# Four attention layers on one core: seven exponential buffers, key tiles of 512, and a new order of the side work

## The chip, the core and the metric

The kernel runs on one core of one Trainium2 chip. The metric is the device time of one execution in microseconds (us). Five engines work side by side, each through its own instructions in a fixed order: TensorE (PE in the profile, its weight loads apart as PEld) multiplies matrices into PSUM, ScalarE (ACT) computes the exponentials, VectorE (DVE) and GpSimd (POOL) do elementwise work, and SyncE (SP) issues the DMA transfers. Engines wait for each other by semaphores.

## What is computed

Four residual layers over x of 2048 rows and 512 columns, with 32 heads of 16 columns. Layers 0 and 2 see a window of 256 keys, layers 1 and 3 see all 2048 keys.

```python
qkv = (layernorm(x) @ wqkv).reshape(B, S, 3, H, Dh)      # H = 32, Dh = 16, S = 2048
scores = einsum("bhqd,bhkd->bhqk", q, k) * Dh ** -0.5     # window layers: 0 <= q - k < 256, else -1e9
o = einsum("bhqk,bhkd->bhqd", softmax(scores), v)
x = x + o.reshape(B, S, D) @ wo                           # A (window), B (full), A, B
```

## The kernel before

**Attention.** A layer is cut into four chunks of 512 queries (index `c`) and eight groups of four heads (`qd`, called a quad here). In a full layer a quad walks over 16 tiles `j` of 128 keys, and each tile is done in two halves `pr` of two heads: 32 steps to a quad, 1,024 to a full layer. A step is one call of `exps` (L748): eight matmuls of scores into one of two PSUM tiles `s` (L758), and one ScalarE exponential of 128x1024 numbers into a tile `e` from a pool of `EB` = 6 buffers (L762, L763). What the exponentials are multiplied with comes later: `attn_full` (L795) hands out closures `pv`, two for each `j`, each of 16 matmuls with the values into the accumulators `acc` (L808). Both closures of a `j` read both of its `e` tiles, so the two tiles come free when the second closure is done. `flush(n)` (L766) issues closures until only `n` are left; L801 sets how far they lag:

```python
flush(2 - pr + (1 if n == 3 or 12 <= n < 20 else 2 if 4 <= n < 12 else 0))
```

`n` is the step in the quad. The lag is longer at the start of a quad, since the accumulators have first to be emptied by DVE's two transposes of `epilogue` (L723, L726). The call of `flush` stands behind `exps` in each step, and so do its matmuls in TensorE's order.

**Side work.** Projections of keys and queries for later layers or chunks, values, and output projections are written as generators, wrapped in `Work` objects, and fed into the steps by `Side.share` (L975). TensorE's order is exactly the order in which the program issues; nothing reorders it later. The planner keeps a clock of its own (`spent`, `clock`), a time `PH["free"]` before which no side unit may go on, and a budget for each step. In full layers a side unit is a run of `mms` (L421): up to 12 pairs of 64-row matmuls into the one PSUM pair `PH["pair"]`, a piece to a step as a rule. Side.one (L927) picks the first work in the queue that is ready.

**Squares' sums.** After a projection of keys or queries (`keys` L577, `queries` L589) DVE joins the two PSUM halves and splits the result (L451, L452, L542, L543), POOL squares it (L548), and TensorE sums the squares by heads (`squares`, L568); DVE takes the maximum (L586) for keys or makes a row `m` for queries (L599, L600), and `m` goes to DRAM (L613), to the query tiles that are loaded later (L776). The TensorE part is put off: it is appended to `pend` with a due time 3.6 us later on the planner's clock. But in a full layer `mms` settles all of `pend` whenever the next unit begins, due or not (L424 to L427). At the end of each chunk `settle()` (L1046) does the same.

**Layer 3** is done in four passes `t` of two quads, each over the four chunks: 16 sections of 64 steps. `side3(t, c)` (L1182) lists what is done beside a section: the next chunk's queries of this pass (`Q3`), the next pass's keys of this chunk (`K3`), the output projection of the section before (`O3`), parts of the values (`upper`); in the last section of a pass also `shift3` (the key maximum of the next pass, which settles `pend` and writes a row of the keys) and the next pass's first queries. `Side.finish` (L986) issues what is left at the section's end without steps between.

**Loads.** `load_full` (L772) brings the next quad's queries `qt` (2 buffers) and its keys as two tiles `kt` of 1024 keys (3 buffers); `load_win` (L784) does it for the window layers. The schedule of every engine but TensorE is made at build time from priorities and from when a buffer should come free.

Of the kernel before, what the change touches and what calls it, by code (L numbers as in the profile page):

```python
# [31 lines left out]
MM = 0.222  # L32
HEAD_START = 100
HQ = QC // 2
EB, XB, XNB, WB, VB, OB = 6, 4, 4, 2, 3, 5
L_MIN = 2.0 ** -90
L_SUM = 2.0 ** 60

# [149 lines left out]
def fast_path(ctx, tc, flag, a_x, a_wqkv, a_wo, b_wqkv, b_wo, out):  # L188
# [214 lines left out]
    def phase(l):  # L403

        PH["full"], PH["win"] = l is not None and l % 2 == 1, l is not None and l % 2 == 0
        if PH["full"] or not PH["win"] and "pool" not in PH or l is None and PH.get("pair"):
            ps_x.close()
            PH["pool"] = ps_x.enter_context(tc.tile_pool(name=f"ps_x{l}", bufs=1 if PH["full"] else 2, space=bass.MemoryType.PSUM))
            PH["room"] = 0.0
            PH["pair"] = PH["pool"].tile([P, 2, QC], F32, name=f"s{l}") if PH["full"] else None  # L410

    def bank(halves=False):
# [5 lines left out]
            return ps_s.tile([P, 2, QC], F32, name=f"bs{turn['bank']}", tag="s")[:, 0, :]  # L418
        return PH["pool"].tile([P, QC], F32, name=f"b{turn['bank']}", tag="b")

    def mms(ps, pairs, after=1.6, us=MM):  # L421


        if PH["full"] and pend:  # L424
            settle()
            PH["free"] = clock[0] + 2.2
            yield 0.1  # L427
        for i, (a, b) in enumerate(pairs):
            if PH["full"]:
                for g in range(0, P, 32):  # L430
                    for r in range(2):
                        half = slice(R * r, R * r + R)
                        nc.tensor.matmul(ps[g:g + 32, r], a[half, g:g + 32], b[half], start=(i == 0),  # L433
                                         stop=(i == len(pairs) - 1), skip_group_check=True)
            else:
                nc.tensor.matmul(ps, a, b, start=(i == 0), stop=(i == len(pairs) - 1))  # L436
            spent(us)
            if i < len(pairs) - 1:
                if PH["full"]:
                    yield us  # L440
            else:
                PH["free"] = clock[0] + (1.7 if PH["full"] else after)
    TERMS = ((0, 0), (0, 1), (1, 0))

    def joined(n, ps, rows=slice(0, P)):
# [66 lines left out]
    def project(l, s, c, act, ht=None, first=None):  # L512


        ty, n = l % 2, f"{l}_{s}_{c}" + ("" if ht is None else f"_h{ht}")
        if not first:
            w = weights(ty, s, n, *((0, D) if ht is None else (ht * P, (ht + 1) * P)))
            yield wait(8)
            xc = XC[l, c]
        if s == 0:  # L520
            dst = rows(qs[ty, c])
        elif ty == 0:
            dst = rows(kw[c])
        else:
            dst = rows(kf)[:, :, c * QC:(c + 1) * QC]
        sqs = {}
        for t in range(NHT) if ht is None else (ht,):
            ps = bank(True)
            w0 = t * P if ht is None else 0
            if first:  # L530
                yield from mms(ps, [(first[0][:, k, t * P:(t + 1) * P], first[1][:, k, :]) for k in range(NC)])
            else:
                yield from mms(ps, [(w[:, k, a, w0:w0 + P], xc[:, b, k, :]) for k in range(NC) for a, b in TERMS], 2.2)
            settle(not sqs)
            ps = joined(f"{n}_{t}", ps)
            sp = vp.tile([P, 2, QC], F16, name=f"sp{n}_{t}", tag="sp", bufs=3)
            e = first[2][:, t:t + 1] if first else es[:, ty, s, t:t + 1]
            with tc.high_priority(HEAD_START):
                if act:
                    nc.scalar.activation(sp[:, 0], ps, AF.Copy, scale=e)  # L540
                else:
                    nc.vector.tensor_scalar(sp[:, 0], ps, e, None, op0=ALU.mult)  # L542
                nc.vector.scalar_tensor_tensor(sp[:, 1], ps, e, sp[:, 0], op0=ALU.mult, op1=ALU.subtract)  # L543
            sq = vp.tile([P, QC], BF16, name=f"sq{n}_{t}", tag="sq", bufs=NHT)
            if act:
                nc.scalar.activation(sq, sp[:, 0], AF.Square)
            else:
                nc.gpsimd.tensor_tensor(sq, sp[:, 0], sp[:, 0], ALU.mult)  # L548
            sqs[t] = sq

            d = dst[8 * t:8 * t + 8].rearrange("h (d b) n -> (h d) b n", b=4)
            if s:
                nc.sync.dma_start(d[:, 0:2], sp[:, 0:1].broadcast_to([P, 2, QC]))
                nc.sync.dma_start(d[:, 2], sp[:, 1])
            else:
                nc.sync.dma_start(d[:, 0:2], sp)
                nc.sync.dma_start(d[:, 2], sp[:, 0])
            yield -MM if PH["full"] else -12 * MM
        return sqs
# [185 lines left out]
            ONR[l, c, t] = clock[0] + 4.5  # L745


    def exps(name, kt, qt, pr, pieces):  # L748

        turn["s"] += 1  # L750
        ps = ps_s.tile([P, 2, QC], F32, name=f"s{name}", tag="s")
        w0 = min(p[3] for p in pieces)
        w1 = max(p[3] + p[2] for p in pieces)
        for kc, qc, wd_, s0 in pieces:
            for g in range(0, P, 32 if PH["full"] else P):
                for h in range(2):
                    out_ = slice(g, g + 32) if PH["full"] else slice(0, P)
                    nc.tensor.matmul(ps[out_, h, s0:s0 + wd_], kt[R * h:R * h + R, pr, kc + out_.start:kc + out_.stop],  # L758
                                     qt[R * h:R * h + R, pr, qc:qc + wd_], start=True, stop=True,
                                     skip_group_check=PH["full"])  # L760
        spent(0.22 if PH["full"] else 0.27)
        e = pp.tile([P, 2, QC], F32, name=f"e{name}", tag="e", bufs=EB)  # L762
        nc.scalar.activation(e[:, :, w0:w1], ps[:, :, w0:w1], AF.Exp, scale=SCALE)  # L763
        return e
# [7 lines left out]
    def load_full(l, c, qd):  # L772
        n = f"{l}_{c}_{qd}"
        pair = slice(2 * qd, 2 * qd + 2)
        qt = pp.tile([P, 2, QC], F16, name=f"qt{n}", tag="qt", bufs=2)
        nc.sync.dma_start(qt, qs[1, c][pair].rearrange("r p n -> p r n"))  # L776
        kts = []
        for v in range(2):
            kt = pp.tile([P, 2, S // 2], F16, name=f"kt{n}_{v}", tag="kt", bufs=3)
            nc.sync.dma_start(kt, kf[pair, :, v * S // 2:(v + 1) * S // 2].rearrange("r p n -> p r n"))  # L780
            kts.append(kt)
        return kts, qt

    def load_win(l, c, qd):  # L784
        n = f"{l}_{c}_{qd}"
        kt = pp.tile([P, 2, S // 2], F16, name=f"kt{n}", tag="kt", bufs=3)
        qt = pp.tile([P, 2, QC], F16, name=f"qt{n}", tag="qt", bufs=2)
        pair = slice(2 * qd, 2 * qd + 2)
        nc.sync.dma_start(qt, qs[0, c][pair].rearrange("r p n -> p r n"))
        nc.sync.dma_start(kt[:, :, WIN:WIN + QC], kw[c][pair].rearrange("r p n -> p r n"))  # L790
        if c:
            nc.sync.dma_start(kt[:, :, :WIN], kw[c - 1][pair, :, QC - WIN:].rearrange("r p n -> p r n"))
        return kt, qt

    def attn_full(l, c, qd, kt, qt, a):  # L795
        for j in range(NT):
            es_ = []
            for pr in range(2):
                es_.append(exps(f"{l}_{c}_{qd}_{j}_{pr}", kt[j // 8], qt, pr, [(j % 8 * P, 0, QC, 0)]))
                n = 2 * j + pr  # L800
                flush(2 - pr + (1 if n == 3 or 12 <= n < 20 else 2 if 4 <= n < 12 else 0))  # L801
                PH["side"](-0.18 if n in (12, 20) else 0.68 if n in (3, 4) else 0.25)
# [15 lines left out]
    def attn_win(l, c, qd, kt, qt, a):  # L818
        first = True
        for u, tiles in enumerate(WTILES):  # L820
            tiles = [p for p in tiles if c or p[0] >= 0]
            es_ = []
            for pr in range(2):
                e = exps(f"{l}_{c}_{qd}_{u}_{pr}", kt, qt, pr,
                         [(WIN + j * P, q * P, nb * P, s * P) for j, q, nb, s in tiles])
                ev = e.rearrange("p h (m n) -> p h m n", n=P)
                edges = [(s + b, q + b - j == 2) for j, q, nb, s in tiles for b in range(nb) if q + b - j != 1]
                for b, far in edges:
# [82 lines left out]
    class Side:  # L911
# [15 lines left out]
        def one(self, force=False):  # L927

            if force:
                self.prefetch()  # L930
            at = [(w.ready_at(), i) for i, w in enumerate(self.q)]
            at = [(r, i) for r, i in at if r is not None]
            now = [i for r, i in at if r <= clock[0]]
# [7 lines left out]
            return self.piece(self.q[i])  # L941

        def piece(self, w):
            c = w.advance()
            if c is None:
                self.q.remove(w)
                return 0.0
            self.spent += abs(c)
            return c
# [231 lines left out]

    def side3(t, c):  # L1182
        a = [Q3(c + 1, t)] if c < 3 else []
        if t < 3:
            a.append(K3(c, t + 1))
            if c == 3:
                a += [shift3(t + 1), Q3(0, t + 1)]
        if (t, c) != (0, 0):
            a.append(O3(c - 1, t) if c else O3(3, t - 1))
        if t < 2 and (t or c > 1):  # L1190
            a.insert(0, upper(3, 2 * t + c // 2, range(2 * (c % 2), 2 * (c % 2) + 2)))
        return a
# [55 lines left out]
```

## Time and profile before

| | us |
|---|---|
| the runs of the kernel before, median (lowest) | 2910.45 (2908.99) |
| the profiled execution | 2904.52 |
| its span, first to last instruction | 2902.8 |
| ACT busy in the span | 2403.3 |
| PE busy in the span | 2615.5 |

The profiled execution is 5.9 us below the median and 1.7 us above its own span. A row of the timeline merges instructions of one line on one engine that follow each other with less than 0.15 us of idle time: it has the start, the time from the first start to the last end, and the count; in brackets stands the idle time before it and what ended that. A row of the waits has the engine and line that waited, what ended the wait, the sum in us, the number of waits and the longest one.

### The profile page before, as it was taken

The page shows a single profiled execution, that of the slowest core. Times are in us where ns is not written, and L with a number is a line of the kernel's source. Part 1 is how long each engine was busy: PE and PEld are TensorE (multiplying, and loading weights), DVE is VectorE, ACT ScalarE, POOL GpSimd, SP SyncE. Part 2 cuts the span into 40 slices and gives each one's busy share as a digit, 9 for nine tenths or more (in the row PEclk, how much of TensorE's full clock was granted, in tenths as well). Part 3 has the DMA queues.
Part 4 walks back from the last instruction along what each step waited for, and adds up shares of the span by engine and source line. Part 5 has one row for each costly group of instructions (what it writes and reads, how often), then busy time and mean ns, then how long its engine had stood idle before and what let it go on. Part 6 is the DMA issues. An engine that isn't in the chain of part 4 may idle for free.

```text
span 2902.8 us, 145250 instructions
## 1 busy us (share of the span) xinstructions
PE 2615.5 (90%) x66941; PEld 1361.8 (47%) x66941; DVE 1223.0 (42%) x2496; ACT 2403.3 (83%) x2687; POOL 588.6 (20%) x1129
## 2 busy tenths in 40 slices
PE   8899999989999999999898899889888888889987
PEld 4333344555545554555453334545555454444443
DVE  7678654112332233222336667223444334343333
ACT  3566663999999999999995765699899889999997
POOL 3577660001001000000015776000000000000000
PEclk9999999999999999999999999999999999999999
DMA  6877676122232223222326644423333433233331
GB/s 223 219 242 218 198 231 199 54 68 89 86 101 77 71 86 96 82 73 77 102 90 192 174 144 140 137 72 95 107 101 106 121 96 107 91 104 102 101 99 55
DMA packets 317836, 350.24 MB, mean 121 GB/s; under 512 B 113056, under 2 KB 233376, under 8 KB 311200
## 3 DMA queue, kind: packets, MB, share of 16 engines
q1 hardware_dynamic: 317216, 340.86, 38.4%
q8 instruction: 525, 8.60, 1.2%
q14 instruction: 95, 0.78, 0.1%
HBM read 228.07 MB, written 96.99 MB: 112 GB/s over the span
## 4 chain that ended last, share of the span: by engine, by line
ACT 40%; PE 35%; issue 11%; DVE 7%; POOL 4%; DMA 2%; SPq 0%; ACTq 0%; POOLq 0%; DVEq 0%
ACT e L763 39%; PE acc L808 9%; PE b L436 9%; PE s L758 8%; PE acc L842 3%; PE s L433 3%; PE bs L436 1%; POOL sq_h L548 1%; POOL wr L345 1%; POOL e L832 1%; POOL e L835 1%; DVE xh L483 0%; DVE xh L477 0%; DVE xn L477 0%; PE s L568 0%
## 5 line engine op out<-in xcount | busy, mean ns | idle before, releaser
L763 ACT ACTIVATE e<-s 128x1024 f32<-128x1024 f32 (+2 forms) x2432 | 2269.8, 1047 | 215.7 <-PE s L758 155.5
L808 PE MATMUL acc<-e,vt 64*17 64x256 f32 x32768 | 1326.1, 378 | 24.4 <-issue 18.2
L758 PE MATMUL s<-qt,kt 64*32 64x512 f16 (+3 forms) x17792 | 1032.5, 376 | 161.4 <-ACT e L763 103.5
L758 PEld LDWEIGHTS <-kt 64*32 64x32 f16 (+1 forms) x17792 | 457.0, 90 | 799.2 <-issue 630.5
L808 PEld LDWEIGHTS acc<-e,vt 64*17 64x17 f32 x32768 | 606.1, 93 | 188.8 <-issue 38.4
L835 POOL TENSOR_SCALAR_AFFINE_SELECT e<-e 128x256 f32<-128x256 f32 x512 | 228.2, 454 | 124.7 <-ACT e L763 124.1
L744 POOL TENSOR_TENSOR oh<-o,oh 128x512 f16<-128x512 f32 x31 | 36.2, 1168 | 935.6 <-DVE oh L743 890.8
L723 DVE STREAM_TRANSPOSE ot<-acc 128x512 f32<-128x512 f32 x128 | 91.1, 712 | 314.4 <-PE acc L808 244.9
L832 POOL TENSOR_SCALAR_AFFINE_SELECT e<-e 128x256 f32<-128x256 f32 x448 | 198.2, 449 | 74.4 <-ACT e L763 72.2
L842 PE MATMUL acc<-e,vt 128*17 128x384 f32 (+2 forms) x2816 | 203.3, 393 | 5.9 <-POOL e L832 3.8
L436 PE MATMUL b<-xc,w 128*128 128x512 f16 x672 | 156.8, 384 | 9.2 <-DVE sp L543 7.5
L451 DVE COPY jo<-s 128x512 f32<-128x512 f32 x72 | 49.6, 689 | 250.6 <-PE s L433 250.6
L548 POOL TENSOR_TENSOR sq_h<-sp_h 128x512 bf16<-128x512 f16 x27 | 40.1, 1484 | 539.7 <-PE s L758 339.6
L433 PE MATMUL s<-xc,w_h 64*32 64x512 f16 x2592 | 138.8, 381 | 4.5 <-DVE km L586 4.5
L433 PE MATMUL s<-xc,w 64*32 64x512 f16 x2688 | 140.7, 378 | 1.3 <-DVE j L452 1.3
L433 PE MATMUL s<-wv,xc 64*32 64x256 f16 (+1 forms) x3456 | 134.7, 306 | 6.5 <-issue 6.3
L433 PE MATMUL s<-wo,oh 64*32 64x512 f16 x2592 | 135.0, 378 | 4.6 <-DVE jo L452 4.6
L451 DVE COPY j_h<-s 128x512 f32<-128x512 f32 x27 | 18.6, 689 | 285.3 <-PE s L433 285.3
L666 DVE COPY vt<-s 128x256 f32<-128x256 f32 (+1 forms) x36 | 18.4, 512 | 268.2 <-PE s L433 268.1
L451 DVE COPY j<-s 128x512 f32<-128x512 f32 x28 | 19.3, 689 | 258.2 <-PE s L433 258.2
L548 POOL TENSOR_TENSOR sq<-sp 128x512 bf16<-128x512 f16 x28 | 41.4, 1477 | 408.2 <-DVE sp L542 246.8
L436 PEld LDWEIGHTS <-w 128*128 128x128 f16 x720 | 67.2, 98 | 105.1 <-issue 32.4
(180 smaller groups left out, 2074.9 us busy)
## 6 DMA issues: line engine op xcount, KB each, us to landing
kt<-kf SPq DMA_DIRECT2D x128, 512.0 KB
qt<-qs SPq DMA_DIRECT2D x128, 256.0 KB
xd<-x SPq DMA_DIRECT2D x96, 256.0 KB
x<-xd SPq DMA_DIRECT2D x96, 256.0 KB
w<-wd SPq DMA_DIRECT2D x20, 1024.0 KB
kt<-kw SPq DMA_DIRECT2D x64, 256.0 KB
qs<-sp SPq DMA_DIRECT2D x48, 256.0 KB
wo<-wd SPq DMA_DIRECT2D x12, 1024.0 KB
```

The lines of the kernel that those rows point to most:

```text
L433: nc.tensor.matmul(ps[g:g + 32, r], a[half, g:g + 32], b[half], start=(i == 0), stop=(i == len(pairs) - 1), skip_group_check=True)
L436: nc.tensor.matmul(ps, a, b, start=(i == 0), stop=(i == len(pairs) - 1))
L451: nc.vector.tensor_copy(j[rows], ps[rows, 0])
L548: nc.gpsimd.tensor_tensor(sq, sp[:, 0], sp[:, 0], ALU.mult)
L723: nc.vector.transpose(ot.rearrange("p b r -> p (b r)"), a)
L744: (nc.gpsimd if l % 2 and (l, c, qd) != (3, NQ - 1, NQD - 1) else nc.vector).tensor_tensor(hl[:, 1], o, hl[:, 0], ALU.subtract)
L758: nc.tensor.matmul(ps[out_, h, s0:s0 + wd_], kt[R * h:R * h + R, pr, kc + out_.start:kc + out_.stop], qt[R * h:R * h + R, pr, qc:qc + wd_] ...
L763: nc.scalar.activation(e[:, :, w0:w1], ps[:, :, w0:w1], AF.Exp, scale=SCALE)
L808: nc.tensor.matmul(acc[r][32 * h:32 * h + DH + 1, HQ * q:HQ * q + HQ], V[l, qd // 4, j // 8][half, j % 8, 4 * (qd % 4) + h, :], es_[h // 2 ...
L832: nc.gpsimd.affine_select(v, v, pattern=[[0, 2], [-1, P]], compare_op=ALU.is_gt, fill=0.0, base=0, channel_multiplier=1)
L835: nc.gpsimd.affine_select(v, v, pattern=[[0, 2], [1, P]], compare_op=ALU.is_ge, fill=0.0, base=0, channel_multiplier=-1)
L842: nc.tensor.matmul(a[32 * h:32 * h + DH + 1, q * P:(q + nb) * P], V[l, (4 * c + j) // 4][:, j % 4, 4 * qd + h, :], es_[h // 2][:, h % 2, s ...
```

## The change

Four edits:

1. `EB` goes from 6 to 7: seven tiles for the exponentials.
2. The keys of a full layer are loaded as four tiles of 512 (4 buffers) and not as two of 1024 (3 buffers). A window layer's 768 keys take two tiles, or one at chunk 0.
3. `mms` settles `pend` only when its last entry is due on the planner's clock, or when the unit is the first one of a projection (`must`); in the second case, if it is not due yet, side work is first held back until it is. `PH["unit"]` names the work whose unit is begun, and `Side.one` goes on with it until its last matmul.
4. `side3` puts `O3` ahead of `K3`, and in the last section of a pass between `K3` and `shift3`.

```diff
-EB, XB, XNB, WB, VB, OB = 6, 4, 4, 2, 3, 5
+EB, XB, XNB, WB, VB, OB = 7, 4, 4, 2, 3, 5
...
-    def mms(ps, pairs, after=1.6, us=MM):
-        if PH["full"] and pend:
-            settle()
-            PH["free"] = clock[0] + 2.2
-            yield 0.1
+    def mms(ps, pairs, after=1.6, us=MM, must=False):
+        if PH["full"]:
+            if pend and must and pend[-1][0] > clock[0]:
+                PH["free"] = max(PH["free"], pend[-1][0])
+                yield 0.0
+            if pend and (must or pend[-1][0] <= clock[0]):
+                settle()
+                PH["free"] = clock[0] + 2.2
+                yield 0.1
+            PH["unit"] = PH["now"]
...
-                yield from mms(ps, [(w[:, k, a, w0:w0 + P], xc[:, b, k, :]) for k in range(NC) for a, b in TERMS], 2.2)
+                yield from mms(ps, [(w[:, k, a, w0:w0 + P], xc[:, b, k, :]) for k in range(NC) for a, b in TERMS], 2.2, must=not sqs)
...
-        for v in range(2):
-            kt = pp.tile([P, 2, S // 2], F16, name=f"kt{n}_{v}", tag="kt", bufs=3)
-            nc.sync.dma_start(kt, kf[pair, :, v * S // 2:(v + 1) * S // 2].rearrange("r p n -> p r n"))
+        for v in range(4):
+            kt = pp.tile([P, 2, QC], F16, name=f"kt{n}_{v}", tag="kt", bufs=4)
+            nc.sync.dma_start(kt, kf[pair, :, v * QC:(v + 1) * QC].rearrange("r p n -> p r n"))
...
+            if PH["unit"] in self.q:
+                return self.piece(PH["unit"])
...
         a = [Q3(c + 1, t)] if c < 3 else []
+        o = [] if (t, c) == (0, 0) else [O3(c - 1, t) if c else O3(3, t - 1)]
         if t < 3:
-            a.append(K3(c, t + 1))
+            a += ([] if c == 3 else o) + [K3(c, t + 1)]
             if c == 3:
-                a += [shift3(t + 1), Q3(0, t + 1)]
-        if (t, c) != (0, 0):
-            a.append(O3(c - 1, t) if c else O3(3, t - 1))
+                a += o + [shift3(t + 1), Q3(0, t + 1)]
+        else:
+            a += o
```

No arithmetic, type or size of a matmul or an exponential changes.

More of the change, by code (lines that the diff above doesn't have):

```diff
@@ L408, in phase @@
             PH["pool"] = ps_x.enter_context(tc.tile_pool(name=f"ps_x{l}", bufs=1 if PH["full"] else 2, space=bass.MemoryType.PSUM))
-            PH["room"] = 0.0
+            PH["room"], PH["unit"], PH["now"] = 0.0, None, None
             PH["pair"] = PH["pool"].tile([P, 2, QC], F32, name=f"s{l}") if PH["full"] else None
@@ L441, in mms @@
             else:
-                PH["free"] = clock[0] + (1.7 if PH["full"] else after)
+                PH["free"], PH["unit"] = clock[0] + (1.7 if PH["full"] else after), None
     TERMS = ((0, 0), (0, 1), (1, 0))
@@ L745, in epilogue, with exps @@
             ONR[l, c, t] = clock[0] + 4.5
-    def exps(name, kt, qt, pr, pieces):
+    def exps(name, qt, pr, pieces):
         turn["s"] += 1
         ps = ps_s.tile([P, 2, QC], F32, name=f"s{name}", tag="s")
-        w0 = min(p[3] for p in pieces)
-        w1 = max(p[3] + p[2] for p in pieces)
-        for kc, qc, wd_, s0 in pieces:
+        w0 = min(p[4] for p in pieces)
+        w1 = max(p[4] + p[3] for p in pieces)
+        for kt, kc, qc, wd_, s0 in pieces:
             for g in range(0, P, 32 if PH["full"] else P):
@@ L785, in load_win @@
         n = f"{l}_{c}_{qd}"
-        kt = pp.tile([P, 2, S // 2], F16, name=f"kt{n}", tag="kt", bufs=3)
+        kt = [pp.tile([P, 2, QC], F16, name=f"kt{n}_{v}", tag="kt", bufs=4) for v in range(2 if c else 1)]
         qt = pp.tile([P, 2, QC], F16, name=f"qt{n}", tag="qt", bufs=2)
@@ L789, in load_win @@
         nc.sync.dma_start(qt, qs[0, c][pair].rearrange("r p n -> p r n"))
-        nc.sync.dma_start(kt[:, :, WIN:WIN + QC], kw[c][pair].rearrange("r p n -> p r n"))
+        nc.sync.dma_start(kt[0], kw[c][pair].rearrange("r p n -> p r n"))
         if c:
-            nc.sync.dma_start(kt[:, :, :WIN], kw[c - 1][pair, :, QC - WIN:].rearrange("r p n -> p r n"))
+            nc.sync.dma_start(kt[1][:, :, :WIN], kw[c - 1][pair, :, QC - WIN:].rearrange("r p n -> p r n"))
         return kt, qt
@@ L798, in attn_full @@
             for pr in range(2):
-                es_.append(exps(f"{l}_{c}_{qd}_{j}_{pr}", kt[j // 8], qt, pr, [(j % 8 * P, 0, QC, 0)]))
+                es_.append(exps(f"{l}_{c}_{qd}_{j}_{pr}", qt, pr, [(kt[j // 4], j % 4 * P, 0, QC, 0)]))
                 n = 2 * j + pr
@@ L823, in attn_win @@
             for pr in range(2):
-                e = exps(f"{l}_{c}_{qd}_{u}_{pr}", kt, qt, pr,
-                         [(WIN + j * P, q * P, nb * P, s * P) for j, q, nb, s in tiles])
+                e = exps(f"{l}_{c}_{qd}_{u}_{pr}", qt, pr,
+                         [(kt[j < 0], (j + 2 * (j < 0)) * P, q * P, nb * P, s * P) for j, q, nb, s in tiles])
                 ev = e.rearrange("p h (m n) -> p h m n", n=P)
@@ L943, in piece @@
         def piece(self, w):
+            PH["now"] = w
             c = w.advance()
```

## The prediction

> **What bounds the kernel now.** I read the page first, then the exponentials by stage, then their waits, then single steps.
>
> ```profile
> span 2902.8 us, 145250 instructions
> PE 2615.5 (90%) x66941; PEld 1361.8 (47%) x66941; DVE 1223.0 (42%) x2496; ACT 2403.3 (83%) x2687; POOL 588.6 (20%) x1129
> ACT 40%; PE 35%; issue 11%; DVE 7%; POOL 4%; DMA 2%; SPq 0%; ACTq 0%; POOLq 0%; DVEq 0%
> ```
>
> ACT leads the chain that ended last. PE shows more busy time, but its matmuls overlap, so whether PE is full must be read from who waits for whom. The two full layers, cut at their first and last exponential (row: stretch, its length, ACT's time on L763, count):
>
> ```profile
> 505.30:1511.90 1006.60, 958.41 (x1024) 1.00 0.26 81
> 1844.40:2884.40 1040.00, 959.77 (x1024) 0.99 0.32 97
> ```
>
> They are 2047 of 2903 us, and ACT is busy 95% and 92% of them. So these two stages decide, and in them the spacing of the exponentials. The last passes of layer 3 show it with little beside it:
>
> ```profile
> 2667.38 7.44 ACT L763 ACTIVATE e<-s 128x1024 f32<-128x1024 f32 x8 [0.97 <-PE s L758]
> 2675.41 52.99 ACT L763 ACTIVATE e<-s 128x1024 f32<-128x1024 f32 x56 [0.59 <-PE acc L808]
> 2729.37 7.44 ACT L763 ACTIVATE e<-s 128x1024 f32<-128x1024 f32 x8 [0.96 <-PE s L758]
> 2737.40 52.94 ACT L763 ACTIVATE e<-s 128x1024 f32<-128x1024 f32 x56 [0.59 <-PE acc L808]
> ```
>
> Eight in 7.44 us, with 1.02 for the last, is (7.44-1.02)/7 = 0.917 a step. At that pace 1024 take 939 us: layer 1 has 68 us on top, layer 3 has 101. The runs of 56 go at (52.99-1.02)/55 = 0.945, so they hide idle time too short for the view. The named waits of ACT, layer 1 first, then layer 3:
>
> ```profile
> ACT e L763 <- PE s L758: 24.4, 33, 1.7
> ACT e L763 <- PE acc L808: 12.6, 11, 4.9
> ...
> ACT e L763 <- PE s L758: 50.8, 50, 3.9
> ACT e L763 <- PE acc L808: 20.1, 25, 2.5
> ```
>
> A wait costs its idle time and about 0.10 more, since unhindered exponentials overlap by 1.02-0.917. Layer 1: 37.0+44x0.10 = 41.4 of the 68 named, 27 not. Layer 3: 70.9+75x0.10 = 78.4 of 101, 23 not. The unnamed 50 us are to be explained; the next fence does it (positions 6, 7, 8 and 9 of a quad of 32 steps).
>
> ```profile
> 2674.46 0.41 PE L758 MATMUL s<-qt,kt 64*32 64x512 f16 x8
> 2674.67 0.63 PE L808 MATMUL acc<-e,vt 64*17 64x256 f32 x16
> 2675.41 1.02 ACT L763 ACTIVATE e<-s 128x1024 f32<-128x1024 f32 x1 [0.59 <-PE acc L808]
> 2676.33 1.02 ACT L763 ACTIVATE e<-s 128x1024 f32<-128x1024 f32 x1
> 2676.49 0.41 PE L758 MATMUL s<-qt,kt 64*32 64x512 f16 x8 [0.32 <-ACT e L763]
> 2676.70 0.63 PE L808 MATMUL acc<-e,vt 64*17 64x256 f32 x16
> 2677.44 1.02 ACT L763 ACTIVATE e<-s 128x1024 f32<-128x1024 f32 x1
> 2678.36 1.02 ACT L763 ACTIVATE e<-s 128x1024 f32<-128x1024 f32 x1
> ```
>
> At 2677.44 the scores were ready at 2676.90, yet the exponential starts 0.11 after the value matmuls ended (2677.33): it waited for an `e` buffer. By L801, for n from 4 to 11 an even step leaves four closures queued, which hold four tiles; the two of the `j` before are freed only by the closure issued behind this step's scores. Six are taken, and the step needs a seventh. So steps 6, 8, 10 and 12 of every quad stall: 1.11 against 0.92 here, 0.19 lost, more at step 6. 4x64 = 256 such steps at 0.19 are 49 us, which is the unnamed 50.
>
> **The change, part by part; the sum is made against the profiled execution, 2904.5 us, 5.9 below the median 2910.45.**
>
> *Seven buffers.* The stalling step gets its tile at once; the next, odd one would be the eighth, but its scores stand in PE's order behind the closure that frees two. The 50 us can go. Of the named waits on L808 (36, 32.7 us) each can lose at most one step's lead, 0.92: from the gaps one by one, 14.5 us in layer 3 and 7.8 in layer 1, with the 0.10 each 26. Upper end 76. What is late next is PE: after a longer stop the scores are late as well, and the wait only changes its name. PE's own waits for ACT tell what room it has (layer 3, then layer 1):
>
> ```profile
> PE s L758 <- ACT e L763: 34.7, 96, 1.0
> PE s L568 <- POOL sq_h L548: 32.2, 26, 2.6
> PE s L433 <- DVE km L586: 4.5, 4, 1.3
> ...
> PE s L758 <- ACT e L763: 29.4, 86, 0.9
> PE s L568 <- POOL sq L548: 5.8, 6, 1.5
> ```
>
> 34.7+29.4 = 64 us of named room. I take -62; ends -40 (waits renamed, some of the short ones PE's own, at step 21) and -76.
>
> *Squares' sums behind other units.* 32 times PE stands before L568 until POOL is done, 38.0 us; one event:
>
> ```profile
> 2139.74 0.69 DVE L451 COPY j_h<-s 128x512 f32<-128x512 f32 x1 [13.07 <-PE s L433]
> 2141.85 1.51 POOL L548 TENSOR_TENSOR sq_h<-sp_h 128x512 bf16<-128x512 f16 x1 [25.28 <-PE s L758]
> 2143.41 0.39 PE L568 MATMUL s<-sq_h,hsum 64*32 64x512 bf16 x2 [1.27 <-POOL sq_h L548]
> 2144.15 17.38 ACT L763 ACTIVATE e<-s 128x1024 f32<-128x1024 f32 x18 [1.07 <-PE s L758]
> ```
>
> From the unit's end (2139.7) to the squares 3.7 us; PE waits 1.27 of it and ACT loses 1.07. So 32 x (1.0+0.1) = -35 if all go. They go where another unit runs in between: Q3, O3, K3 in place of Q3, K3, O3, the sums falling in at O3's second unit. The DVE wait of 1.3 behind `shift3` goes in two of four sections, -3. Three things come back. First, K3 is now last in a section, and `settle()` at the section's end does not wait for a due time: where K3 ends within 3.7 us of it, PE stands there. Six or seven sections are full enough (an estimate from how late their last pieces stand); the output projection's last piece there is forced today, and costs this:
>
> ```profile
> 2174.70 0.84 PE L433 MATMUL s<-wo,oh 64*32 64x512 f16 x24 [0.89 <-DVE jo L452]
> 2175.89 2.86 ACT L763 ACTIVATE e<-s 128x1024 f32<-128x1024 f32 x3 [1.24 <-PE s L758]
> ```
>
> I take +6 net. Second, in the last section of a pass the next pass's first queries now end the list, and the next section's first scores wait for their `m`, its DMA and the query load. Today 14 us of O3 cover that:
>
> ```profile
> 2087.56 0.41 PE L433 MATMUL s<-xc,w_h 64*32 64x512 f16 x8
> 2093.57 0.29 SPq L613 DMA_DIRECT2D qs<-m  x1
> 2094.88 0.54 SPq L776 DMA_DIRECT2D qt<-qs  x1
> 2107.32 0.41 PE L433 MATMUL s<-wo,oh 64*32 64x512 f16 x8
> 2109.90 0.52 PE L433 MATMUL s<-wv,xc 64*32 64x256 f16 x24
> ```
>
> Unit end to query load is 2094.88-2087.9 = 7 us, about 3 for the load to land (estimate: a 512 KB key load took 4.58, row below; this one is half), 0.5 for the scores: 10.5. The side work ends about 0.5 before the section does today; one settlement (2.3 on the planner's clock) falls away, so some 2.7 remain, and ACT has 1.5 of scores in hand: 6 us are left open. By the queue's order it happens at the end of the first and second pass; in the third the free weight slot goes to the queries first, O3 comes last as now, and the old stall stays. 2x6 = +12. Third, a held-back projection (`must`) costs PE nothing, only side time. Sum of this part -35-3+6+12 = -20; ends -38 and +5.
>
> *Units finished first.* One PSUM pair serves all side units, so two begun units never could mix; this guards the new order and costs nothing. Ends -1 and +1.
>
> *Four key tiles.* They pay for the seventh buffer's room. 128 more DMA issues of about 0.4 us lie on SP, which no engine waits for today. The next quad's tile v now waits for this quad's step 8v+7, and is needed 24 steps later, 22 us; the cover is that lead. SP is in order, so stores and weight loads placed behind such an issue wait with it:
>
> ```profile
> SPq L780 <- PE s L758: 483.6, 56, 15.0
> ...
> 1839.27 4.58 DMA kt<-kf
> ...
>   DMA kt<-kf: 0.3, 1
> ```
>
> (SP's own waits; the key load that the chain of waits has at the start of layer 3; what PE waited for on the tile kt.) SP stands so up to 15 us today, and PE lost 0.3 us to these loads. I take 0; ends -3 (a first tile that lands sooner) and +15. In the window layers both key tiles come free with the query tile, which already had two buffers and whose issue stands ahead of them: 0, ends -3 and +6.
>
> The trace shows key loads hidden. The Trainium skill speaks against this edit: "DMA: Bandwidth & Descriptors", Rules for kernel authors, wants at least 1 MiB per DMA, and "SBUF — State Buffer", The DMA setup-cost knee, gives each transfer some 2 us that do not shrink with it. By it, as an estimate, 128 more transfers in series would cost 256 us; by the rows, nothing while the lead covers them.
>
> Sum: 2904.5-62-20+0 = 2822; with the 5.9 to the median, 2828.
>
> **The rivals.**
>
> *PE takes over.* Seven buffers only rename the waits and the squares' gain is half lost. For it: PE has as much named idle time (64 us) as I want to take back, and side pieces come in bursts. Against: that idle time lies at the very steps that stall (2676.49 above). -40-5+8 for window and SP noise: 2910-37 = 2873.
>
> *The section ends eat the squares' gain.* If every K3 settles late (9 sections x 2.5 = +22 for +6) and the query load opens 10 us three times (+30 for +12): -62-35-3+22+30 = -48, so 2862.
>
> *Exposed key loads, the slower one.* If stores or keys queued behind a waiting key issue come late, PE stands at quad starts, 64 of them. 2910-82 = 2828 turns into no gain at 82/64 = 1.3 us a quad; at 3 us, under one 4.58 us load, it is +192-82 = +110: 3020. Over 2.2 us a quad it is slower by more than 2%. Against: the 22 us lead. It is what the rule of the Trainium skill on small transfers ("DMA: Bandwidth & Descriptors", above) would lead to here; its chance is this rival's.
>
> *More goes than I credit.* All 76, all 35, section ends free: 2910-76-38-3 = 2793.
>
> **How the numbers follow.** Forecast 0.62, PE takes over 0.14, section ends 0.10, exposed loads 0.06, more 0.08. The time is the forecast's. A measurement of this kernel tells about 2% from no change, so faster means under 2852, slower over 2969. The forecast's own range is 2800 to 2855, 0.61 of its 0.62 faster, and "more" is faster: 0.69. PE takes over, section ends and 0.01 each of the forecast and the exposed loads are within: 0.26. Slower is the rest of the exposed loads: 0.05. The range from 2785 to 2878 leaves out the exposed loads and the outer ends of "more" and "PE takes over".
>
> **What would show it.** Right: single exponentials at steps 8, 10 and 12 follow at 0.92, runs of 56 take about 51.5 us, ACT's waits on L808 fall from 32.7 to under 12, PE's wait before L568 from 38 to under 12, layer 1 takes about 970 us and layer 3 about 990. Wrong: ACT's waits on L758 grow by what those on L808 lose (PE took over); gaps of over 5 us at pass starts behind a query load, or waits before L568 at section ends (section ends); PE waiting for `kt` or weights (key loads). A window layer that moves by over 10 us would be something I do not see.

## The result and the profile after

| | before | after |
|---|---|---|
| median of the runs (lowest to highest of after) | 2910.45 | 2891.49 (2887.54 to 2891.72) |
| ratio, 95% interval | | 0.993 [0.9914, 0.9945] |
| profiled execution, its span | 2904.52, 2902.8 | 2891.49, 2889.7 |

One of the five executions of the kernel before took 5811.91 us, twice the others; the record does not say why, and the median is not moved by it.

The change makes the kernel 0.7% faster. The forecast was 2828, with a range from 2785 to 2878; the time lies 13 us above the range. The gain is 19 us where 82 were forecast. The page of after, then its two full layers cut at their first and last exponential (stretch, length, ACT's time on the exponentials and their count, PE's granted clock, DMA share, GB/s):

```profile
span 2889.7 us, 145534 instructions
ACT 41%; PE 33%; issue 11%; DVE 8%; DMA 4%; POOL 2%; SPq 1%; ACTq 0%; POOLq 0%; DVEq 0%
```

```profile
510.70:1490.40 979.70, 948.51 (x1024) 0.99 0.28 84
1825.70:2871.30 1045.60, 953.00 (x1024) 0.97 0.32 97
```

ACT still leads the chain, and DMA has doubled its share of it (2% to 4%). Layer 1 fell from 1006.6 to 979.7, by 27 of the 37 us forecast (970). Layer 3 was to fall from 1040 to 990 and rose to 1045.6: of the 65 us that the two layers lack, 55 lie there and 10 in layer 1. Layer 3's granted clock, 0.99 before, is 0.97. The waits of after, layer 1 above the dots and layer 3 below (engine and line that waited, what ended it: us, times, longest):

```profile
ACT e L768 <- PE s L763: 28.8, 36, 4.3
...
ACT e L768 <- PE s L763: 89.7, 70, 12.7
PE s L573 <- POOL sq_h L553: 23.7, 7, 3.7
PE s L763 <- DMA qt<-qs: 21.8, 3, 8.1
```

ACT's waits for values, 32.7 us before, are gone from both layers: no such row is left. PE's wait before the squares' sums is gone from layer 1 and down to seven events in layer 3, but these are long ones, 23.7/7 = 3.4 us each where 26 of them took 1.2. A row that was not there before is PE's wait for the query tile `qt`. And ACT's waits on scores in layer 3 went from 50.8 to 89.7. They sit in a few places. The seven longest stops of layer 3 (the timeline of ACT, idle time in brackets):

```profile
2016.69 1.02 ACT L768 ACTIVATE e<-s 128x1024 f32<-128x1024 f32 x1 [4.26 <-PE s L763]
2090.32 1.02 ACT L768 ACTIVATE e<-s 128x1024 f32<-128x1024 f32 x1 [10.23 <-PE s L763]
2157.47 2.02 ACT L768 ACTIVATE e<-s 128x1024 f32<-128x1024 f32 x2 [3.90 <-PE s L763]
2225.21 1.02 ACT L768 ACTIVATE e<-s 128x1024 f32<-128x1024 f32 x1 [4.39 <-PE s L763]
2295.58 1.02 ACT L768 ACTIVATE e<-s 128x1024 f32<-128x1024 f32 x1 [6.66 <-PE s L763]
2369.95 1.02 ACT L768 ACTIVATE e<-s 128x1024 f32<-128x1024 f32 x1 [12.73 <-PE s L763]
2628.20 1.02 ACT L768 ACTIVATE e<-s 128x1024 f32<-128x1024 f32 x1 [7.98 <-PE s L763]
```

Each is the first exponential of a section. Three open a pass (10.23, 12.73, 7.98: 30.9 us); four open a section inside a pass (4.26, 3.90, 4.39, 6.66: 19.2 us). The first pass start, step by step (DVE joins the last unit's halves, POOL squares, PE sums, SP writes `m` and loads the queries, PE makes scores):

```profile
2079.55 0.69 DVE L456 COPY j_h<-s 128x512 f32<-128x512 f32 x1 [10.54 <-PE s L438]
2081.66 1.51 POOL L553 TENSOR_TENSOR sq_h<-sp_h 128x512 bf16<-128x512 f16 x1 [30.82 <-DVE sp_h L547]
2083.22 0.61 PE L573 MATMUL s<-sq_h,hsum 64*32 64x512 bf16 x2 [3.73 <-POOL sq_h L553]
...
2085.30 0.28 SPq L618 DMA_DIRECT2D qs<-m  x1
2086.67 0.89 SPq L781 DMA_DIRECT2D qt<-qs  x2
2089.57 0.63 PE L763 MATMUL s<-qt,kt 64*32 64x512 f16 x8 [5.74 <-DMA qt<-qs]
```

From the unit's end to the query load 7.1 us, and 10.0 to the scores: what the prediction worked out. But the unit ends with the section, not some 4 us ahead of it, so nothing covers the chain: ACT runs out at 2080.09, 0.5 us after the unit's end, and loses 10.23 us. PE stands 3.73 and 5.74 us of it.

### The profile page after: what moved, and what is told of

Its sections match the earlier page's. It is cut to its first block, busy times and chain, and to the rows that moved or that the text cites. A ratio compares the mean times of both kernels' runs of the same rounds, so it can differ in the third digit from the quotient of the medians.

```text
span 2889.7 us, 145534 instructions
## 1 busy us (share of the span) xinstructions
PE 2604.8 (90%) x66941; PEld 1383.0 (48%) x66941; DVE 1215.6 (42%) x2496; ACT 2386.0 (83%) x2687; POOL 588.8 (20%) x1129
## 4 chain that ended last, share of the span: by engine, by line
ACT 41%; PE 33%; issue 11%; DVE 8%; DMA 4%; POOL 2%; SPq 1%; ACTq 0%; POOLq 0%; DVEq 0%
ACT e L768 40%; PE acc L813 9%; PE b L441 9%; PE s L763 7%; PE s L438 4%; PE acc L847 3%; PE bs L441 1%; DMA kt<-kw 1%; DMA qt<-qs 1%; POOL e L837 1%; POOL wr L345 1%; DVE xh L488 1%; POOL e L840 0%; DVE sp L548 0%; DVE xn L482 0%
## 5 line engine op out<-in xcount | busy, mean ns | idle before, releaser
L813 PE MATMUL acc<-e,vt 64*17 64x256 f32 x32768 | 1352.5, 379 | 23.4 <-issue 17.3
L763 PE MATMUL s<-qt,kt 64*32 64x512 f16 (+3 forms) x17792 | 1050.4, 377 | 166.3 <-ACT e L768 86.9
L813 PEld LDWEIGHTS acc<-e,vt 64*17 64x17 f32 x32768 | 622.8, 93 | 203.0 <-issue 48.0
L438 PE MATMUL s<-xc,w_h 64*32 64x512 f16 x2592 | 153.2, 376 | 4.6 <-issue 2.7
L438 PE MATMUL s<-wv,xc 64*32 64x256 f16 (+1 forms) x3456 | 141.0, 311 | 2.6 <-issue 2.5
```

What stands on the lines that cost most here:

```text
L813: nc.tensor.matmul(acc[r][32 * h:32 * h + DH + 1, HQ * q:HQ * q + HQ], V[l, qd // 4, j // 8][half, j % 8, 4 * (qd % 4) + h, :], es_[h // 2 ...
```

## The experiments

Three theories stood against each other. A: the buffers and the later settlement gain, and the new side order gives it back at section ends and pass starts. B: PE has taken over, so that a seventh buffer gains little whatever the order. C: the four key tiles cost what the others gain. The kernel before had a median of 2913.46 beside the first four kernels and of 2912.13 beside the last four; ratios are to these.

Executions of one kernel differ by up to 24 us (2836.08 to 2856.25 in e1_side_old, 2917.6 to 2937.38 in e3_eb6, 2833.57 to 2857.27 in e8_best), and in these three the profiled execution lies at one end of the range. So a difference of medians and a difference of two traces need not agree to 10 us.

### The old order of the side work (e1_side_old)

```diff
         a = [Q3(c + 1, t)] if c < 3 else []
-        o = [] if (t, c) == (0, 0) else [O3(c - 1, t) if c else O3(3, t - 1)]
         if t < 3:
-            a += ([] if c == 3 else o) + [K3(c, t + 1)]
+            a.append(K3(c, t + 1))
             if c == 3:
-                a += o + [shift3(t + 1), Q3(0, t + 1)]
-        else:
-            a += o
+                a += [shift3(t + 1), Q3(0, t + 1)]
+        if (t, c) != (0, 0):
+            a.append(O3(c - 1, t) if c else O3(3, t - 1))
```

> The changed kernel with the old list of side work in layer 3 (queries, keys, output projection; in a pass's last section keys, shift3, queries, output projection). Theory A (the seventh buffer and the sums inside a section gained some 75 us, and the new places of the section-closing units gave 48 of it back at layer 3's section starts): layer 3 falls from 1044 to about 1000 us, step 0 of the sections loses under 10 us instead of 54, the profiled time is about 2847. Rival B (TensorE is the bound, and the waits at the section starts are only its backlog): the idle time turns up elsewhere and the time stays between 2880 and 2895.

Measured: 2849.04, ratio 0.9789 [0.9767, 0.9811]. Without edit 4 the kernel is 42 us faster than after. Its two layers:

```profile
502.20:1482.00 979.80, 948.96 (x1024) 0.99 0.28 84
1814.90:2816.40 1001.50, 951.14 (x1024) 1.00 0.34 101
```

Its waits in layer 3:

```profile
ACT e L768 <- PE s L763: 47.7, 49, 5.4
...
PE s L573 <- POOL sq_h L553: 3.5, 3, 1.5
```

Layer 1, which has no side order of this kind, is that of after (979.8 to 979.7). Layer 3 is 44.1 us shorter, and ACT's waits on scores are 42.0 less. Most of it is at the section starts: the seven stops of after are 50.1 us, and here four are left, 2.61, 2.72, 5.44 and 5.21, 16.0 us in all. Theory A had expected under 10. The longest, and the waits of PE that go with all four:

```profile
2197.05 6.52 ACT L768 ACTIVATE e<-s 128x1024 f32<-128x1024 f32 x7 [5.44 <-PE s L763]
...
PE s L438 <- DVE jo L457: 10.0, 6, 1.9
```

At these four section ends PE issues the last two or three pieces of the output projection one after the other, with no steps between, and waits each time until DVE has emptied the PSUM pair.

PE's wait for the squares is down to 3.5 us with the old order. So edit 3 removed these waits by itself; edit 4 was not needed for it.

### Before with the seventh buffer and four key tiles (e2_eb_kt)

```diff
-EB, XB, XNB, WB, VB, OB = 6, 4, 4, 2, 3, 5
+EB, XB, XNB, WB, VB, OB = 7, 4, 4, 2, 3, 5
...
-        for v in range(2):
-            kt = pp.tile([P, 2, S // 2], F16, name=f"kt{n}_{v}", tag="kt", bufs=3)
+        for v in range(4):
+            kt = pp.tile([P, 2, QC], F16, name=f"kt{n}_{v}", tag="kt", bufs=4)
...
```

> The kernel before with seven exponential buffers and the four key tiles alone. Theory A: steps 6, 8, 10 and 12 of a quad stop stalling; layer 1 about 983 us (1006 before), layer 3 about 1008 (1040), window layers 7 more; profiled time about 2856. Rival B: the buffers only rename waits, 2895 to 2910.

Measured: 2862.16, ratio 0.9821 [0.98, 0.9841]. Edits 1 and 2 alone bring 51 us. B (2895 to 2910) and C (a loss) both fall as they were put; how much of B is in the result is read from the next but one experiment.

### After with six buffers (e3_eb6)

```diff
-EB, XB, XNB, WB, VB, OB = 7, 4, 4, 2, 3, 5
+EB, XB, XNB, WB, VB, OB = 6, 4, 4, 2, 3, 5
```

> The changed kernel with six exponential buffers again. Theory A: layer 1 about 1003 us and layer 3 about 1075, so 2946 in all, slower than before the change. Rival B: 2890 to 2900, the seventh buffer was worth nothing.

Measured: 2924.52, ratio 1.0037 [1.0024, 1.005]. The seventh buffer is worth 33 us in the kernel after (2924.52 to 2891.49; the ten executions with six buffers lie between 2917.6 and 2937.38). The direction is A's; the size, 55 in the expectation, is not.

### Before with four key tiles alone (e4_kt)

The edit is that of e2_eb_kt without its first two lines.

> The kernel before with the four key tiles alone (six exponential buffers). Theory A with the window layers' loss put down to the key tiles: full layers as before, layer 0 about 5 us and layer 2 about 2 us longer, 2912 profiled. Rival C (the key tiles and what queues behind their loads ate the gain): over 2925. If they cost nothing: 2904.

Measured: 2896.77, ratio 0.9939 [0.992, 0.9959]. The key tiles gain 17 us by themselves, which no theory had. With e2_eb_kt it isolates the seventh buffer once more: 2896.77 to 2862.16, 35 us. What becomes of the waits shows why it is not 62. The waits of e4_kt, six buffers, layer 1 and layer 3:

```profile
ACT e L763 <- PE s L758: 17.5, 25, 1.5
ACT e L763 <- PE acc L808: 12.6, 9, 5.4
...
ACT e L763 <- PE s L758: 49.3, 52, 3.8
ACT e L763 <- PE acc L808: 15.4, 24, 1.9
```

The waits of e2_eb_kt, seven buffers, layer 1 and layer 3:

```profile
ACT e L763 <- PE s L758: 34.2, 50, 4.5
...
ACT e L763 <- PE s L758: 63.2, 73, 3.8
```

The waits on values (28.0 us) are gone, and the waits on scores are 30.6 us more: the named part only changed its name. The gain is all in what has no name. The layers of e4_kt, then of e2_eb_kt:

```profile
506.50:1505.90 999.40, 957.72 (x1024) 1.00 0.27 82
1841.70:2879.30 1037.60, 962.06 (x1024) 0.99 0.33 97
```

```profile
503.50:1490.80 987.30, 950.67 (x1024) 0.99 0.28 83
1827.40:2845.90 1018.50, 953.02 (x1024) 0.99 0.33 99
```

Less 939 for 1024 steps at 0.917 and less the named waits with 0.10 each, e4_kt has 26.9 and 26.3 us unnamed, e2_eb_kt 9.1 and 9.0: 35 us less. The 0.917 is itself a little slow for an unhindered step. The last exponential of the prediction's run of eight, in the kernel before, took 1.09 us and not 1.02:

```profile
2673.72 1.09 ACT L763 ACTIVATE e<-s 128x1024 f32<-128x1024 f32 x1
```

So the eight went at (2673.72-2667.38)/7 = 0.906 a step. At that pace each sum of unnamed time, here and in the prediction, is 11 us a layer larger; the differences between kernels stay. Where there is little side work, the stall's end is plain. The run of e2_eb_kt that stands in the place of the prediction's 52.99 (after a stop of 0.59):

```profile
2641.51 51.90 ACT L763 ACTIVATE e<-s 128x1024 f32<-128x1024 f32 x56 [0.17 <-PE s L758]
```

That is 1.5 us less in 64 steps, or 48 in the 2048 of both layers. Where side work is dense, part of it came back, as the starts of all the exponentials in the two traces show. Of the 256 steps 6, 8, 10 and 12, 255 begin more than 1.0 us after the step before in e4_kt, and 29 in e2_eb_kt. Over 0.904 a step, the median, these steps lose 83 us in e4_kt and 26 in e2_eb_kt: 57 less. All other steps lose 102 us, and then 128: 26 more.

### Settling only what is due inside a pass (e5_settle_due)

```diff
                 if not win:
-                    settle()
+                    settle(l == 1 or c == NQ - 1)
```

At the end of a section inside a pass of layer 3 only sums that are due are issued; the others wait for the next section's first units.

> The changed kernel, but at the end of a section of layer 3 (not the last of a pass) only sums that are due are settled; a key unit that has just ended carries its sums into the next section. Theory A: the stops before steps 0 of the sections inside a pass (4.3, 3.9, 4.4, 6.7 us, 19 in all) shrink to the forced rest of the key unit, some 4 in all; the three at pass starts (31 us) stay; layer 3 about 1029 us, 2876 profiled. If TensorE were simply late there (rival B), no change.

Measured: 2876.67, ratio 0.9874 [0.9857, 0.989], layer 3 1031.8 us. The four stops at section ends are gone (at most 1.02 us is left), the three at pass starts stay, with 10.68, 10.16 and 11.06 us:

```profile
2088.74 1.02 ACT L768 ACTIVATE e<-s 128x1024 f32<-128x1024 f32 x1 [10.68 <-PE s L763]
...
2615.34 1.02 ACT L768 ACTIVATE e<-s 128x1024 f32<-128x1024 f32 x1 [11.06 <-PE s L763]
```

### The old order in the last section of a pass alone (e6_c3_old)

```diff
             if c == 3:
-                a += o + [shift3(t + 1), Q3(0, t + 1)]
+                a += [shift3(t + 1), Q3(0, t + 1)] + o
```

> The changed kernel with the old order in the last section of a pass alone (keys, shift3, queries, output projection). Theory A: the stops of 10.2, 12.7 and 8.0 us at the pass starts go (-31), the wait of shift3 for POOL comes back (+3 in each of two passes), the stops at the other section ends stay: layer 3 about 1020 us, 2867 profiled. Rival B: no change.

Measured: 2863.81, ratio 0.9833 [0.9817, 0.985], layer 3 1026.5 us. The mirror image: the four at section ends stay (4.58, 4.34, 4.39 and 6.99 us; the last is shown), and the longest at a pass start is 0.40, in the second row:

```profile
2291.89 1.02 ACT L768 ACTIVATE e<-s 128x1024 f32<-128x1024 f32 x1 [6.99 <-PE s L763]
...
2357.42 5.61 ACT L768 ACTIVATE e<-s 128x1024 f32<-128x1024 f32 x6 [0.40 <-PE s L763]
```

The two experiments take apart the 42 us of edit 4: 15 us at section ends (2891.49 to 2876.67) and 28 at pass starts (to 2863.81).

### Both, and `shift3` held back (e7_both), and the values' part behind the keys (e8_best)

e7_both has the edits of e5_settle_due and e6_c3_old, and `shift3` waits 4 us on the planner's clock, since its own settlement follows K3 directly:

```diff
         def gen():
+            yield wait(4)
             key_shift(3, ht)
```

> Both of the two mends at once, and shift3 held back 4 us on the planner's clock so that TensorE does not stand before POOL. Theory A: the gains add up, layer 3 about 1000 us, 2846 profiled. Rival B: 2880 or more.

Measured: 2851.78, ratio 0.9796 [0.9773, 0.9819], layer 3 1004.6 us: the two gains add up, as theory A had it. e8_best goes on from it; in the last section of a pass the part of the values stands behind K3, and so between K3 and `shift3`:

```diff
         if t < 2 and (t or c > 1):
-            a.insert(0, upper(3, 2 * t + c // 2, range(2 * (c % 2), 2 * (c % 2) + 2)))
+            a.insert(c == 3, upper(3, 2 * t + c // 2, range(2 * (c % 2), 2 * (c % 2) + 2)))
```

> As the last one, and in the last section of a pass the value unit runs between keys and shift3, so that no unit there is held back. Theory A: layer 3 about 995 us, 2841 profiled, faster than the changed kernel by 1.7% and than the kernel before by 2.2%. Rival B: 2880 or more.

Measured: 2839.11, ratio 0.977 [0.9736, 0.9804]. Its layers:

```profile
505.50:1484.50 979.00, 948.65 (x1024) 1.00 0.28 84
1817.50:2813.30 995.80, 951.40 (x1024) 1.00 0.34 101
```

This is 2.3% below the kernel before and, by medians taken at different times, 1.8% below after. Stops of 3.11, 3.62 and 1.20 us are left at the pass starts. Its interval overlaps that of e1_side_old (0.9789), so the order of edit 4, mended, is not shown to be better than the old one.

## Why the prediction was wrong, point by point

Three terms of the sum failed, by about 25 us each. The first is the side order: "2x6 = +12" for the pass starts, with "in the third the free weight slot goes to the queries first, O3 comes last as now, and the old stall stays", and "+6 net" for the section ends. Edit 4 measured +42 (e1_side_old to after) in place of +18. The second is "I take -62" for the seventh buffer, which measured -35. The third is the squares' sums, -38, with "a held-back projection (`must`) costs PE nothing, only side time"; they measured -13. One gain, of the key tiles, was not expected. By medians, one edit at a time:

| step | forecast | measured | between |
|---|---|---|---|
| four key tiles | 0 (-3 to +15) | -17 | before, e4_kt |
| seventh buffer | -62 (-40 to -76) | -35; -33 | e4_kt, e2_eb_kt; e3_eb6, after |
| sums when due (edit 3) | -35 -3 | -13 | e2_eb_kt, e1_side_old |
| side order (edit 4) | +6 +12 | +42 | e1_side_old, after |
| sum | -82 | -22 | beside a before of 2913.46 |

The row of edit 3 is the least sure: by the two runs' intervals it is -13 with some 9 us either way.

**Pass starts.** The mechanism and its length were right (10.0 us for 10.5 at the first pass start), and it was the cover that was misjudged: the prediction took 2.7 us of freed side time and 1.5 us of scores in hand off a chain of 10.5. In the trace the unit ends with the section and the chain is bare. The third pass start went wrong in another way. O3 does come last there, but the queries' sums wait behind it:

```profile
2597.60 1.51 POOL L553 TENSOR_TENSOR sq_h<-sp_h 128x512 bf16<-128x512 f16 x1 [17.17 <-PE s L763]
...
2613.26 0.69 DVE L456 COPY jo<-s 128x512 f32<-128x512 f32 x1 [2.20 <-PE s L438]
...
2619.11 0.38 PE L573 MATMUL s<-sq_h,hsum 64*32 64x512 bf16 x2
...
2624.51 0.89 SPq L781 DMA_DIRECT2D qt<-qs  x2
2627.44 0.63 PE L763 MATMUL s<-qt,kt 64*32 64x512 f16 x8 [7.95 <-DMA qt<-qs]
```

The squares were ready at 2599.1 and the sums ran at 2619.1, at the section's end, with all of O3 in between. With the old list in the last section alone (e6_c3_old) the stop is gone. The code's reason (argued from the code): the sums enter `pend` in the projection's closing call, and O3 stands ahead of it in the queue after its last matmul. In e8_best, with O3 behind the queries in the list, the same sums run 2.4 us after the squares are ready, some 10 us ahead of the pass start at 2571.24:

```profile
2556.69 1.52 POOL L553 TENSOR_TENSOR sq_h<-sp_h 128x512 bf16<-128x512 f16 x1 [18.75 <-PE s L763]
2560.56 0.38 PE L573 MATMUL s<-sq_h,hsum 64*32 64x512 bf16 x2
```

**Section ends.** "Where K3 ends within 3.7 us of it, PE stands there" happened in four sections, with stops of 3.90 to 6.66, not 2.5. This was the rival "the section ends eat the squares' gain": its +22 and +30 are close to the 19.2 and 30.9 of the rows. It gave 2862, since it kept the full -62 and -35.

**Seventh buffer.** The mechanism is right: ACT's waits for values are gone, and 57 us went at the steps that stalled. The stall was sized as 49 us against an unnamed 50; that match is partly luck, since at 0.906 a step the unnamed time is 72. What failed is the allowance for what comes back. The prediction itself says that "the wait only changes its name" and charged it only in its lower end, -40: at the other steps 26 us came back, and ACT's waits on scores are 30.6 us more. The "64 us of named room" in PE did not prevent it; 45.5 us of PE's waits for ACT (20.6 and 24.9) are still there in e2_eb_kt while ACT waits for scores at other steps. This is the rival "PE takes over": its -40 is near the measured -35 and -33, and "the squares' gain is half lost" came as well, though not only for its reason.

**Squares' sums.** "32 x (1.0+0.1) = -35 if all go": PE's waits before the sums fell from 40.1 us in e2_eb_kt (6.3 and 33.8 by layer) to 3.5 in e1_side_old, which is what was forecast. The time fell by 13 in the medians, and by 24.5 in the two full layers of the traces. Part of the rest was lost in side time, which the prediction put at nothing: the side work that was held back stood at the section ends. Where e1_side_old issues two or three pieces of the output projection there, e2_eb_kt issues one, with less waiting for DVE (10.0 us in e1_side_old, in layer 3):

```profile
PE s L568 <- POOL sq_h L548: 33.8, 26, 2.7
...
PE s L433 <- DVE jo L452: 4.7, 7, 0.9
```

ACT's stops at these four section starts are 1.24 us each in e2_eb_kt, 5.0 in all, and 16.0 in e1_side_old: 11 us of the gain went back there. Which part of edit 3 displaced the pieces was not tried by itself. e8_best is 23 us below e2_eb_kt, but it differs in more than the sums and was measured beside another before.

**Key tiles, units first, window.** Units first was not tried by itself; it is part of the step from e2_eb_kt to e1_side_old. The exposed loads did not happen; no row of PE's waits on `kt` is among those of the full layers. The rule weighed in the prediction, at least 1 MiB a DMA (the Trainium skill, "DMA: Bandwidth & Descriptors", Rules for kernel authors), stands there for the highest bandwidth, and it did not decide the time here: twice as many loads of half the size made the kernel faster, 0.9939 [0.992, 0.9959]. The Trainium skill's "Perfetto Trace Analysis", DMA Optimizations, has a point that fits, that splitting DMAs may let some start sooner; the direction agrees, but which wait the 17 us came out of was not found. The traces show only 5.2 us of them (spans of 2902.8 and 2897.6): layer 1 is 7.2 shorter (1006.6 to 999.4) and layer 3 2.4 (1040.0 to 1037.6), and the stretches around them are 4.4 longer. Layer 1 starts at 510.7 in after and 505.3 in before, but at 502.2 in e1_side_old with the same window code, so these 5 us are not the window's key tiles. PE's waits on the window layers' `kt`, which the prediction put at nothing, went from 2.3 us in before to 6.1 in after.

The chances put 0.62 on a case in which every term came out as worked; as it was, parts of two rivals came together, which no case had.

## What to carry to other kernels

Before work is moved to the end of a stage, follow its whole chain of successors (here: squares, sums, row, DRAM, load, scores, 10 us) and find the work that covers it in the new place by its time in the trace, not by a budget. Work that is held back has to run somewhere: look at where the stage ends. A wait that is removed can come back under another name at other steps, so count the bound's own stops, all of them, before and after. When several edits go in together, a wrong order at seven places (42 us) can cost more than any one of the others gains (35, 17 and 13).

## What the hardware did that was not expected

A stop of PE costs more than its length. The first pass start of after in short stretches (stretch, length, ACT's time and count, granted clock of PE):

```profile
2080.00:2082.00 2.00, 0.09 (x1) 1.00 0.67 193
2082.00:2083.00 1.00, 0.00 (x0) 0.72 1.04 275
...
2091.00:2092.00 1.00, 0.74 (x2) 0.50 0.06 16
2092.00:2093.00 1.00, 0.74 (x2) 0.66 0.00 0
2093.00:2094.00 1.00, 1.00 (x2) 1.00 0.00 0
```

PE stood 3.73 us until 2083.22. A mean of 0.72 from 2082 to 2083 puts the halving of its granted clock at 2082.4, 2.9 us after its last matmul; a mean of 0.66 puts the return at 2092.7, 3.1 us after the scores began at 2089.57. In between eight score matmuls took 0.63 us and not 0.41, and exponentials followed at 1.28 and not 0.92:

```profile
2091.60 1.02 ACT L768 ACTIVATE e<-s 128x1024 f32<-128x1024 f32 x1 [0.26 <-PE s L763]
```

Two exponentials lose 0.36 us each so, 0.7 us on top of the stop. The trace of after has such a stretch at each of the seven stops of layer 3, 58 us at half rate in all, and e1_side_old has none there; so the mean granted clock of the layer is 0.97 and 1.00. The Trainium skill's "TensorE: Matmul & The Clock Gate", Part 1, describes this: the array goes to half rate after an idle window of about 3.4 us and comes back after as long a busy one. The rows come near both, with 2.9 and 3.1 us.
